# Cache rows of 32 KiB instead of 16 KiB: two heads per 4 MiB transfer, softmax and PV by pairs of heads

## The chip, the cores and the metric

One NeuronCore of a Trainium2 chip. The metric is the device time of one execution in microseconds (us), lower is better. Differences of less than 2% count as "same"; most comparisons are read from the traces and from several timed rounds on one chip, with the kernel before run beside each.

## The reference

One decode step: layernorm, attention of one query per batch row over a cache of 8,192 keys for 32 heads, and a feed-forward block, both added to x. Everything is bf16 in HBM.

```python
B, Sq, D = 4, 1, 512;  H, Sk, Dh = 32, 8192, 128;  F = 1792
def _A_ref(x, k_cache, v_cache, wq, wo):           # k_cache, v_cache: [B, H, Sk, Dh]
    q = (x @ wq).reshape(B, Sq, H, Dh).transpose(0, 2, 1, 3)
    scores = einsum("bhqd,bhkd->bhqk", q, k_cache) * (Dh ** -0.5)
    p = softmax(scores, axis=-1)
    o = einsum("bhqk,bhkd->bhqd", p, v_cache)
    return o.transpose(0, 2, 1, 3).reshape(B, Sq, H * Dh) @ wo
def _B_ref(x, w_gate, w_up, w_down):
    return (silu(x @ w_gate) * (x @ w_up)) @ w_down
xn = layernorm(A_x)
return A_x + _A_ref(xn, ...) + _B_ref(xn, ...)
```

K and V are 268 MB each, and each byte is used once. All else is small: 8 MB of projections, 5.5 MB of feed-forward weights.

## The kernel before

K and V come in tiles of 2 MiB, one per (head, batch row). A tile is [128 partitions x 8,192 elements]: partition p holds 64 consecutive keys, so a row of one partition is 16 KiB, contiguous in HBM. Nine buffers of 16 KiB per partition (`slot`) hold tiles of K, V and weights in turn. All loads are issued by SyncE, in program order.

```python
    T = Sk // P          # 64 keys on a partition
    NSLOT = 9
    LP = 4               # PV runs four tiles behind the scores
    nc.sync.dma_start(out=x_sb[:], in_=x_flat[:, :])
    ...                  # wq in two loads of 2 MiB
    def load_k(m):
        h, b = divmod(m, B)
        t_ = slot()
        nc.sync.dma_start(out=t_[:], in_=A_k_cache[b, h, :, :].rearrange("(p t) d -> p (t d)", p=P))
        k_tiles[m] = t_
    ...                  # load_v alike; the last V tile in 4 parts
    def load_wo(half):   # rows of 1 KiB, 16 of them on a partition
        n = H // 2
        t_ = slot()
        nc.sync.dma_start(out=t_[:].rearrange("p (h e) -> p h e", h=n),
                          in_=A_wo[half * n * P:(half + 1) * n * P, :].rearrange("(h p) e -> p h e", p=P))
```

Per K tile VectorE transposes four pieces of 16 keys per partition (laid out by the kernel in blocks of QB = 32 x 32 words), and TensorE takes each turned piece through four matmuls against a query matrix that is zero except in the right columns, so that all scores of a head gather in one PSUM tile of 128 rows x 512. After four tiles (one head) comes the softmax; PV runs for each V tile as 16 matmuls with 4 rows of output and 512 columns.

```python
    def t_piece(m, g):
        w = TG * Dh                                    # TG = 16
        kt = kt_pool.tile([P, w], dt.bfloat16, name="kt")
        src = k_tiles[m][:, g * w:(g + 1) * w].bitcast(dt.uint32)
        nc.vector.transpose(out=..., in_=src.rearrange("p (t j r) -> p t j r", j=2, r=QB))
    def s_piece(m, g):
        ...
        for jp in range(4):
            mm(s_ps[h][:], zq[h % 2][:, b, jp, off:off + P], kt[:, jp // 2, :, jp % 2], ...)
    def pv_chunk(m, k):
        mm(o_acc[h % 2][b * QB:b * QB + NV, :], pt[h][:, s * NV:(s + 1) * NV, 2 * (b * NTG + g)],
           v_tiles[m][:, k * 512:(k + 1) * 512], start=(k == 0))
    ...
    for i in range(M + LP + 1):                        # M = 128 tiles
        if i + 2 < M: load_k(i + 2)
        if 0 <= i + 2 - LP < M: load_v(i + 2 - LP, parts=4 if i + 2 - LP == M - 1 else 1)
        ...                                            # ffn and wo loads at fixed i
        for g in range(NTG): t_piece(i, g); s_piece(i, g)
        ...                                            # softmax, PV of tile i - LP, projection
```

Of the kernel before, what the change touches and what calls it, by code (L numbers as in the profile page):

```python
# [8 lines left out]
dt = mybir.dt  # L9
# [6 lines left out]
def kernel(  # L16
# [20 lines left out]
    assert D % P == 0 and F % P == 0 and Sk == 64 * P  # L37
# [3 lines left out]
    T = Sk // P  # L41
# [6 lines left out]
    NSLOT = 9  # L48
    LP = 4
# [34 lines left out]
    nc.sync.dma_start(out=x_sb[:], in_=x_flat[:, :])  # L84
    wq_v = A_wq.rearrange("(p c) n -> p c n", c=EC)
    wq_t = []
    for c2 in range(0, EC, 2):
        t_ = slot()
        nc.sync.dma_start(out=t_[:].rearrange("p (c n) -> p c n", c=2), in_=wq_v[:, c2:c2 + 2, :])  # L89
        wq_t.append(t_)  # L90
# [3 lines left out]
    def load_k(m):  # L94
        h, b = divmod(m, B)
        t_ = slot()
        nc.sync.dma_start(out=t_[:], in_=A_k_cache[b, h, :, :].rearrange("(p t) d -> p (t d)", p=P))  # L97
        k_tiles[m] = t_

    def load_v(m, parts=1):  # L100
        h, b = divmod(m, B)
        t_ = slot()
        src = A_v_cache[b, h, :, :].rearrange("(p t) d -> p (t d)", p=P)
        w = SLOT // parts
        for i in range(parts):
            nc.sync.dma_start(out=t_[:, i * w:(i + 1) * w], in_=src[:, i * w:(i + 1) * w])
        v_tiles[m] = t_
# [11 lines left out]
    zq = [const.tile([P, B, 4, ZW], dt.bfloat16, name=f"zq{i}") for i in range(2)]  # L119
# [5 lines left out]
    for o_ in o_acc:  # L125
# [4 lines left out]
    rowb = const.tile([P, B], dt.float32, name="rowb")  # L130
    nc.vector.reduce_sum(out=rowb[:], in_=ident_f[:].rearrange("p (a x g r) -> p x a g r", a=NQ, x=B, r=2)[:, :, :, :, 0],
                         axis=AX.XY)
    rowb_q = const.tile([P, B], dt.float32, name="rowb_q")
    nc.vector.tensor_scalar(out=rowb_q[:], in0=rowb[:], scalar1=qscale, scalar2=None, op0=ALU.mult)

# [29 lines left out]
    for c in range(EC):  # L165
        for half in range(NH):
            for cg in range(NQ):
                n0 = (c % 2) * H * Dh + (half * NQ + cg) * 512
                mm(q_ps[half][cg * QB:(cg + 1) * QB, :], xnt_w[:, c, :], wq_t[c // 2][:, n0:n0 + 512], start=(c == 0))
# [28 lines left out]
    def load_ffn():  # L198
        wg_t, wu_t, wd_t = slot(), slot(), slot()
        w = EC * F  # L200
        nc.sync.dma_start(out=wg_t[:, 0:w], in_=B_w_gate.rearrange("(p c) f -> p (c f)", c=EC))
        nc.sync.dma_start(out=wu_t[:, 0:w], in_=B_w_up.rearrange("(p c) f -> p (c f)", c=EC))
        nc.sync.dma_start(out=wd_t[:, 0:FC * D], in_=B_w_down.rearrange("(p c) e -> p (c e)", c=FC))
        ffn["w"] = (wg_t[:, 0:w].rearrange("p (c f) -> p c f", c=EC),
                    wu_t[:, 0:w].rearrange("p (c f) -> p c f", c=EC),
                    wd_t[:, 0:FC * D].rearrange("p (c e) -> p c e", c=FC))
# [26 lines left out]

    wo_t = []

    def load_wo(half):
        n = H // 2
        t_ = slot()
        nc.sync.dma_start(out=t_[:].rearrange("p (h e) -> p h e", h=n),
                          in_=A_wo[half * n * P:(half + 1) * n * P, :].rearrange("(h p) e -> p h e", p=P))  # L240
        wo_t.append(t_)


    kts, s_ps, pt, rcp, nmx, osb = {}, {}, {}, {}, {}, {}
    rs_t = {}

    def build_q(h):
        half, cg, hh = h // 16, (h % 16) // 4, h % 4
        for a in range(NQ):
            nc.vector.tensor_copy(  # L250
                out=zq[h % 2][a * QB:(a + 1) * QB, :, :, XO + a * QB].rearrange("p b (j r) -> p r j b", r=2),
                in_=qt[a * QB:(a + 1) * QB, half, :, hh * 2:hh * 2 + 2, cg * B:(cg + 1) * B])

    def t_piece(m, g):

        w = TG * Dh
        kt = kt_pool.tile([P, w], dt.bfloat16, name="kt")
        src = k_tiles[m][:, g * w:(g + 1) * w].bitcast(dt.uint32)
        nc.vector.transpose(out=kt[:].bitcast(dt.uint32).rearrange("p (j t r) -> p t j r", j=2, r=QB),  # L259
                            in_=src.rearrange("p (t j r) -> p t j r", j=2, r=QB))  # L260
        kts[m, g] = kt

    def s_piece(m, g):
        h, b = divmod(m, B)
        if b == 0 and g == 0:
            s_ps[h] = psS.tile([P, 512], dt.float32, name="sps")
        kt = kts.pop((m, g))[:].rearrange("p (j n r) -> p j n r", j=2, r=2)
        off = XO - 2 * (b * NTG + g)
        for jp in range(4):
            mm(s_ps[h][:], zq[h % 2][:, b, jp, off:off + P], kt[:, jp // 2, :, jp % 2],  # L270
               start=(b == 0 and g == 0 and jp == 0))

    def max_1(h):
        mx = small.tile([P, 1], dt.float32, name="mx")
        nc.vector.reduce_max(out=mx[:], in_=s_ps[h][:], axis=AX.X)  # L275
        nmx[h] = mx

    def max_2(h):

        mps = psM.tile([P, 512], dt.float32, name="mps")  # L280
        nc.tensor.matmul(mps[:, 0:P], lhsT=nmx.pop(h)[:, 0:1].to_broadcast([P, P]), rhs=ident_f[:, :],  # L281
                         is_transpose=True, start=True, stop=True, skip_group_check=True)
        nm = small.tile([P, B], dt.float32, name="nm")
        nc.vector.tensor_reduce(out=nm[:], in_=mps[:, 0:P].rearrange("p (a x g r) -> p x a g r", a=NQ, x=B, r=2)[:, :, :, :, 0],  # L284
                                axis=AX.XY, op=ALU.max, negate=True)
        nc.vector.tensor_tensor(out=nm[:], in0=nm[:], in1=rowb_q[:], op=ALU.mult)
        nb = small.tile([P, 1], dt.float32, name="nb")
        nc.vector.reduce_sum(out=nb[:], in_=nm[:], axis=AX.X)
        p_ = pp.tile([P, 512], dt.bfloat16, name="p_")
        rs = small.tile([P, 1], dt.float32, name="rs")  # L290
        nc.scalar.activation(out=p_[:], in_=s_ps.pop(h)[:], func=ACT.Exp, bias=nb[:, 0:1], scale=qscale,
                             accum_out=rs[:])
        pt[h] = p_
        rs_t[h] = (rs, mps)

    def pt_turn(h):
        t_ = pp.tile([P, TG, QB], dt.bfloat16, name="pt_")
        nc.vector.transpose(out=t_[:].rearrange("p t x -> p (t x)"), in_=pt[h][:])  # L298
        pt[h] = t_

    def row_sums(h):
        rs, mps = rs_t.pop(h)
        mm(mps[:, P:P + B], rs[:, 0:1].to_broadcast([P, P]), rowb[:], start=True)
        r_ = small.tile([P, B], dt.float32, name="rcp")
        nc.vector.reciprocal(out=r_[:], in_=mps[:, P:P + B])  # L305
        rcp[h] = r_

    def pv_chunk(m, k):
        h, b = divmod(m, B)
        g, s = divmod(k, TG // NV)  # L310
        mm(o_acc[h % 2][b * QB:b * QB + NV, :], pt[h][:, s * NV:(s + 1) * NV, 2 * (b * NTG + g)],
           v_tiles[m][:, k * 512:(k + 1) * 512], start=(k == 0))

    def fin_1(h):
        o_sb = pp.tile([P, 512], dt.float32, name="o_sb")
        nc.scalar.copy(out=o_sb[:], in_=o_acc[h % 2][:])  # L316
        osb[h] = o_sb

    def fin_2(h, nb=B):

        o_sb = osb.pop(h)
        xps = psX.tile([P, B], dt.float32, name="xps")
        for u in range(NV):
            mm(xps[:, 0:nb], o_sb[:, u * Dh:(u + 1) * Dh], ident_f[:, u:nb * QB:QB], start=(u == 0))
        return xps

    def fin_3(h, xps):
        nc.vector.tensor_tensor(out=otn[:, h, :], in0=xps[:], in1=rcp.pop(h)[:], op=ALU.mult)  # L328

    def pv_last(xps):  # L330

        h, b = divmod(M - 1, B)
        for t in range(T):
            g, u = divmod(t, TG)
            mm(xps[:, b:b + 1], v_tiles[M - 1][:, t * Dh:(t + 1) * Dh], pt[h][:, u, 2 * (b * NTG + g):2 * (b * NTG + g) + 1],
               start=False)

    def wo_mm(h):
        w = wo_t[h // (H // 2)][:].rearrange("p (h e) -> p h e", e=D)
        for j in range(2):  # L340
            mm(yo_ps[j][0:B, :], otn[:, h, :], w[:, h % (H // 2), j * DH:(j + 1) * DH], start=False)

    NK = T // NV
    R_FFN, R_WO = 9, M - 10
    wo_next, wo_ready = 0, 0
    build_q(0)
    for i in range(M + LP + 1):

        if i + 2 < M:
            load_k(i + 2)  # L350
        if 0 <= i + 2 - LP < M:
            load_v(i + 2 - LP, parts=4 if i + 2 - LP == M - 1 else 1)
# [4 lines left out]
        if i == R_WO - 3:  # L357
            load_wo(0)
        if i == R_WO - 2:
            load_wo(1)  # L360
        hs, bs = divmod(i, B)
        hp = hs - 1
        if i < M:
            for g in range(NTG):
                t_piece(i, g)
                s_piece(i, g)
                if g == 0 and bs == 0 and hp >= 0:
                    pt_turn(hp)
            if bs == B - 2 and hs + 1 < H:
                build_q(hs + 1)  # L370
            if bs == B - 1:
                max_1(hs)
        elif i == M:
            pt_turn(H - 1)
        mp = i - LP
        if mp == M - 1:
            xps = fin_2(H - 1, B - 1)
            pv_last(xps)
            fin_3(H - 1, xps)
            wo_ready = H  # L380
        elif 0 <= mp < M:
            for k in range(NK):
                pv_chunk(mp, k)
                if k == NK // 2 and i < M and bs == B - 1:
                    max_2(hs)
            hv, bv = divmod(mp, B)
# [55 lines left out]
```

## Time and profile before

| | before |
|---|---|
| time, median of 3 runs | 1296.54 us (1296.42 to 1296.56) |
| span in the profile | 1294.7 us |
| DMA, mean over the span | 426 GB/s of 551.5 MB |
| steady rate, 520 to 720 us | 431 GB/s |
| TensorE, VectorE busy | 84%, 54% |
| VectorE idle, waiting for K | 287 us |

A high busy share of TensorE beside a DMA that is always busy is not a contradiction: the kernel has two nearly full resources.

### The profile page before, as it was taken

The numbers are of one execution on the slowest core, as the hardware profiler recorded it, in microseconds if no ns is written. First come the engines' busy times: TensorE is split into PE (matmuls) and PEld (weight loads), VectorE is DVE, ScalarE is ACT, GpSimd is POOL, SyncE is SP. The second block draws the span as 40 slices with busy tenths as digits, with TensorE's granted clock in tenths as the row PEclk, the third lists the DMA queues.
The fourth block names the chain that finished last, engine by engine and source line by source line (L and its number), as shares of the span: only waits on it lengthen the run. The fifth ranks groups of instructions, "written<-read, shape, count | busy, mean of one in ns | idle before, by whom it ended". The sixth has DMA issues, their size and how long they took to land.

```text
span 1294.7 us, 11411 instructions
## 1 busy us (share of the span) xinstructions
PE 1091.8 (84%) x4758; PEld 425.8 (33%) x4758; DVE 693.1 (54%) x887; ACT 48.9 (4%) x103; POOL 5.6 (0%) x11
## 2 busy tenths in 40 slices
PE   5888888888888888887888888888888888886997
PEld 2343333333333333333333333333333333332333
DVE  7635554564555565555555555555555545543552
ACT  1000000000000000000000000000000000000000
POOL 1000000000000000000000000000000000000000
PEclk9999998999999999999999899998999999998999
DMA  9999999999999999999999999999999999999997
GB/s 395 431 429 430 431 429 432 430 431 430 432 431 429 430 431 432 429 430 431 432 430 429 431 432 431 430 431 431 430 431 431 430 430 431 431 402 420 430 432 321
DMA packets 42219, 551.51 MB, mean 426 GB/s; under 512 B 4268, under 2 KB 8376, under 8 KB 8888
## 3 DMA queue, kind: packets, MB, share of 16 engines
q1 hardware_dynamic: 42160, 550.79, 99.7%
q8 instruction: 37, 0.61, 0.2%
q14 instruction: 14, 0.11, 0.0%
q10 hardware_dynamic: 8, 0.00, 0.0%
HBM read 550.77 MB, written 0.00 MB: 425 GB/s over the span
## 4 chain that ended last, share of the span: by engine, by line
DMA 89%; PE 8%; DVE 3%; issue 0%; SPq 0%; ACT 0%; DVEq 0%; ACTq 0%
DMA slot<-in_A_k_cache_dram 86%; PE sps L74 4%; PE oacc L74 3%; DMA slot<-in_A_v_cache_dram 3%; DVE kt L259 3%; PE xps L74 0%; SPq L97 0%; PE mps L281 0%; PE mps L74 0%; SPq L89 0%; DVE otn L328 0%; ACT o_sb L316 0%; DVE pt__4838 L298 0%; DVE pt__6510 L298 0%; DVE pt__4014 L298 0%
## 5 line engine op out<-in xcount | busy, mean ns | idle before, releaser
L259 DVE STREAM_TRANSPOSE kt<-slot 128x1024 uint32<-128x1024 uint32 x512 | 593.5, 1212 | 287.2 <-DMA slot<-in_A_k_cache_dram 287.0
L74 PE MATMUL sps<-kt,zq 128*128 128x512 bf16 x2048 | 569.6, 413 | 181.3 <-DVE kt L259 167.4
L74 PEld LDWEIGHTS <-zq 128*128 128x128 bf16 x2048 | 208.0, 102 | 531.3 <-issue 358.9
L305 DVE RECIPROCAL rcp<-mps 128x4 f32<-128x4 f32 x32 | 5.8, 183 | 162.1 <-PE mps L74 162.1
L275 DVE TENSOR_REDUCE mx<-sps 128x1 f32<-128x512 f32 x32 | 22.1, 692 | 43.0 <-PE sps L74 43.0
L284 DVE TENSOR_REDUCE nm<-mps 128x4 f32<-128x64 f32 x32 | 7.2, 224 | 50.0 <-PE mps L281 50.0
L74 PE MATMUL xps<-ident_f,o_sb 128*128 128x4 f32 (+1 forms) x256 | 33.1, 253 | 0.7 <-ACT o_sb L316 0.7
L74 PEld LDWEIGHTS xps<-ident_f,o_sb 128*128 128x128 f32 x256 | 31.1, 192 | 1.2 <-ACT o_sb L316 1.2
L250 DVE COPY zq<-qt 32x16 bf16<-32x16 bf16 x128 | 23.5, 183 | 1.3
L328 DVE TENSOR_TENSOR otn<-xps,rcp 128x4 bf16<-128x4 f32 x32 | 5.2, 162 | 33.1 <-PE xps L74 33.1
L316 ACT COPY o_sb<-oacc 128x512 f32<-128x512 f32 x32 | 18.8, 586 | 18.0 <-PE oacc L74 17.8
L74 PE MATMUL oacc<-slot,pt__3190 128*4 128x512 bf16 x64 | 14.6, 379 | 0.2 <-DMA slot<-in_A_v_cache_dram 0.2
L74 PE MATMUL oacc<-slot,pt__5662 128*4 128x512 bf16 x64 | 14.6, 379 | 0.1
L74 PE MATMUL oacc<-slot,pt__1336 128*4 128x512 bf16 x64 | 14.6, 379 | 0.0
L74 PE MATMUL oacc<-slot,pt__372 128*4 128x512 bf16 x64 | 14.6, 379 | 0.0
L74 PE MATMUL oacc<-slot,pt__2572 128*4 128x512 bf16 x64 | 14.6, 379 | 0.0
L74 PE MATMUL oacc<-slot,pt__3602 128*4 128x512 bf16 x64 | 14.6, 379 | 0.0
L74 PE MATMUL oacc<-slot,pt__4632 128*4 128x512 bf16 x64 | 14.6, 379 | 0.0
L74 PE MATMUL oacc<-slot,pt__5456 128*4 128x512 bf16 x64 | 14.6, 379 | 0.0
L74 PE MATMUL oacc<-slot,pt__6754 128*4 128x512 bf16 x64 | 14.6, 379 | 0.0
L74 PE MATMUL oacc<-slot,pt__578 128*4 128x512 bf16 x64 | 14.6, 379 | 0.0
L74 PE MATMUL oacc<-slot,pt__1954 128*4 128x512 bf16 x64 | 14.6, 379 | 0.0
(206 smaller groups left out, 639.6 us busy)
## 6 DMA issues: line engine op xcount, KB each, us to landing
slot<-in_A_k_cache_dram SPq DMA_DIRECT2D x128, 2048.0 KB, 37.8
slot<-in_A_v_cache_dram SPq DMA_DIRECT2D x127, 2048.0 KB, 38.8
slot<-in_A_wq_dram SPq DMA_DIRECT2D x2, 2048.0 KB, 9.6
slot<-in_A_wo_dram SPq DMA_DIRECT2D x2, 2048.0 KB, 29.4
slot<-in_A_v_cache_dram SPq DMA_DIRECT2D x4, 512.0 KB, 28.0
slot<-in_B_w_gate_dram SPq DMA_DIRECT2D x1, 1792.0 KB, 35.1
slot<-in_B_w_up_dram SPq DMA_DIRECT2D x1, 1792.0 KB, 34.3
slot<-in_B_w_down_dram SPq DMA_DIRECT2D x1, 1792.0 KB
```

The source lines that it names most:

```text
L74: nc.tensor.matmul(out_ap, lhsT=lhsT, rhs=rhs, start=start, stop=True, skip_group_check=True, **kw)
L250: nc.vector.tensor_copy(out=zq[h % 2][a * QB:(a + 1) * QB, :, :, XO + a * QB].rearrange("p b (j r) -> p r j b", r=2), in_=qt[a * QB:(a + 1 ...
L259: nc.vector.transpose(out=kt[:].bitcast(dt.uint32).rearrange("p (j t r) -> p t j r", j=2, r=QB), in_=src.rearrange("p (t j r) -> p t j r", ...
L275: nc.vector.reduce_max(out=mx[:], in_=s_ps[h][:], axis=AX.X)
L284: nc.vector.tensor_reduce(out=nm[:], in_=mps[:, 0:P].rearrange("p (a x g r) -> p x a g r", a=NQ, x=B, r=2)[:, :, :, :, 0], axis=AX.XY, op= ...
L305: nc.vector.reciprocal(out=r_[:], in_=mps[:, P:P + B])
L316: nc.scalar.copy(out=o_sb[:], in_=o_acc[h % 2][:])
L328: nc.vector.tensor_tensor(out=otn[:, h, :], in0=xps[:], in1=rcp.pop(h)[:], op=ALU.mult)
```

## The change

The intent is to halve the number of packets for the same bytes. A tile becomes two heads of one batch row: each head lies on 64 partitions with 128 keys each, so a partition's row is 32 KiB and a transfer 4 MiB. There are five buffers of 32 KiB instead of nine of 16 KiB. Softmax is now done for two tiles (two heads, two batch rows) at a time, and PV covers both heads in one matmul with 8 rows of output; the weights of the half that does not belong to a head are zeros. Besides: wq comes in one load, wo as seven blocks with rows of 4 KiB and one with rows of 1 KiB, x comes on ScalarE's queue, and the last two V tiles are cut into 4 and 5 pieces so that less work is left after the last byte.

```diff
-    T = Sk // P
+    HT = 2
+    NT = M // HT
+    T = HT * Sk // P
-    NSLOT = 9
-    LP = 4
+    NSLOT = 5
+    LP = 2
...
-    nc.sync.dma_start(out=x_sb[:], in_=x_flat[:, :])
+    nc.scalar.dma_start(out=x_sb[:], in_=x_flat[:, :])
+    wq_t = slot()
+    nc.sync.dma_start(out=wq_t[:], in_=A_wq.rearrange("(p c) n -> p (c n)", c=EC))
...
-        nc.sync.dma_start(out=t_[:], in_=A_k_cache[b, h, :, :].rearrange("(p t) d -> p (t d)", p=P))
+        nc.sync.dma_start(out=t_[:], in_=A_k_cache[b, j * HT:(j + 1) * HT, :, :].rearrange("h (p t) d -> (h p) (t d)", t=T))
...   # load_v alike, with a list of widths
+        n = (NB4 - 1) * 4
+        nc.sync.dma_start(out=t_[:, 0:n * D].rearrange("p (k c e) -> p k (c e)", c=4, e=D),
+                          in_=A_wo[0:n * P, :].rearrange("(k p c) e -> p k (c e)", p=P, c=4))
+        nc.sync.dma_start(out=t_[:, n * D:H * D].rearrange("p (h e) -> p h e", e=D),
+                          in_=A_wo[n * P:H * P, :].rearrange("(h p) e -> p h e", p=P))
...   # softmax by groups of two tiles; probabilities of the two heads turned into ptz, zero elsewhere
+        mm(o_acc[j % 2][b * QB:b * QB + w, :], pt[n // 2][:, off:off + (w - 1) * QB + 1:QB],
+           v_tiles[n][:, k * 512:(k + 1) * 512], start=(k == 0))
...   # fin_1: a masking product and a reduce on VectorE replace four matmuls; fin_q fits wo's 4 KiB rows
-            load_v(i + 2 - LP, parts=4 if i + 2 - LP == M - 1 else 1)
+            load_v(nv, (32, 32, 32, 16, 16) if nv == NT - 1 else (32,) * 4 if nv == NT - 2 else (T,))
...
+            xps = x_tile()
+            pv_last(xps, range(T // 2))
+            fin_2(H // HT - 1, xps, nb=B - 1, start=False)
+            pv_last(xps, range(T // 2, T))
```

## The prediction

The 435.0 GB/s comes from the trace's packet records, and the 45 ns of step 1 from that and the steady 431 GB/s.

> **What bounds the kernel now.** The kernel streams 550.8 MB of K cache, V cache and weights from HBM once, so I read first what the DMA does over the span, then what the chain that ended last is made of. From the page:
>
> ```profile
> DMA  9999999999999999999999999999999999999997
> GB/s 395 431 429 430 431 429 432 430 431 430 432 431 429 430 431 432 429 430 431 432 430 429 431 432 431 430 431 431 430 431 431 430 430 431 431 402 420 430 432 321
> DMA packets 42219, 551.51 MB, mean 426 GB/s; under 512 B 4268, under 2 KB 8376, under 8 KB 8888
> DMA 89%; PE 8%; DVE 3%; issue 0%; SPq 0%; ACT 0%; DVEq 0%; ACTq 0%
> L259 DVE STREAM_TRANSPOSE kt<-slot 128x1024 uint32<-128x1024 uint32 x512 | 593.5, 1212 | 287.2 <-DMA slot<-in_A_k_cache_dram 287.0
> slot<-in_A_k_cache_dram SPq DMA_DIRECT2D x128, 2048.0 KB, 37.8
> ```
>
> The DMA is busy in every slice, the rate is flat at 429 to 432, and 89% of the chain is transfers. VectorE, which turns every K tile, is idle 287 us waiting for K to land: it follows the stream. A 2 MiB load takes 37.8 us from issue to landing, nearly eight times the 4.87 us that it takes alone at 431 GB/s: the queue is seven to eight loads deep. The stream itself is the bound, and only its own overhead, its start and its tail can be shortened. Next, busy time by stretches (columns: length, PE, weight loads, DVE, ACT, POOL, clock, DMA share, GB/s):
>
> ```profile
> 520.00:720.00 200.00, 168.59 (x704) 64.61 (x703) 110.28 (x140) 7.86 (x18) 0.00 (x0) 0.97 1.01 431
> 1150.00:1180.00 30.00, 23.20 (x93) 9.09 (x92) 11.42 (x16) 0.00 (x0) 0.00 (x0) 0.89 1.00 389
> 1280.00:1290.00 10.00, 8.70 (x65) 4.06 (x65) 0.16 (x1) 0.59 (x1) 0.00 (x0) 1.00 0.67 275
> ```
>
> 431 GB/s in the steady part; 389 over 30 us where the output projection's weights (wo, rows of 1 KiB) come in, which costs 30 x 42 / 431 = 2.9 us; a thin end. The issuing queue's timeline around wo shows an issue that is itself held up, which no other part of the steady stream has:
>
> ```profile
> 1127.67 0.39 SPq L239 DMA_DIRECT2D slot<-in_A_wo_dram  x1
> 1131.53 29.59 SPq L97 DMA_DIRECT2D slot<-in_A_k_cache_dram  x1
> 1161.21 0.38 SPq L106 DMA_DIRECT2D slot<-in_A_v_cache_dram  x1
> ```
>
> The K load behind wo takes 29.59 us to issue instead of 0.33, so the queue runs dry for a moment near 1160. Last, the end of the chain:
>
> ```profile
> 1251.38 32.79 DMA slot<-in_A_v_cache_dram
> 1284.17 0.04 issue
> 1284.21 3.63 PE oacc L74 x16
> ...
> 1287.92 0.59 ACT o_sb L316
> 1288.51 0.04 issue
> 1288.56 2.67 PE xps L74 x72
> ```
>
> The last V tile but one lands at 1284.17; then come its PV, the copy, the gather and the last tile's 64 matmuls, ending at 1291.22. The trace's packet records put the last V packet at 1288.8, so the tail after the last byte is 1294.7 - 1288.8 = 5.9 us, because PV of the tile before holds it up.
>
> [...] Its single packet records have medians of 611 ns for 16,384 B, 535 for 14,336 B, 159 for 4,096 B, 46 for 1,024 B and 9 for the 4-byte completion writes. The first four lie on one line: (611 - 46) / (16,384 - 1,024) is 27.19 B per ns, times 16 engines 435.0 GB/s, plus 8.3 ns per packet. [...]
>
> **The change part by part.**
> 1. K, V and the query weights come in 4 MiB transfers of 128 rows of 32 KiB, each engine moving 8 packets for twice the bytes. At 431 GB/s 2 MiB take 4.866 us, at 435.0 they would take 4.821: 45 ns of overhead per 2 MiB for 8 packets and a completion write. (Their records sum to 8 x 8.3 + 9 = 75 ns; consecutive packets overlap a little, so I trust the elapsed figure.) Both halve, to 22 ns per 2 MiB. There are 128 K, 128 V and 2 query loads: 258 x 22.4 ns = 5.8 us saved.
> 2. wo comes as 7 blocks of 4 KiB rows and one of 1 KiB rows: 56 x 159 + 32 x 46 ns = 10.4 us per engine, against 4 MiB at 431 GB/s of 9.7, so 0.7 us is lost instead of 2.9. The queue then holds about 90 descriptors of wo instead of 256 for each half, and I expect no held issue. 2.2 us saved.
> 3. The last two V tiles are cut into 4 and 5 pieces with rows of 8 and 4 KiB; this costs about 0.2 us back.
> 4. x goes to ScalarE's queue, so the first big load is issued one 0.4 us slot earlier: 0.35 us saved.
> 5. Tail: PV of the tile before the last is done as its pieces land, more than 5 us before the end; behind the last piece remain 16 of the 128 closing matmuls. From the rows here: 0.3 landing, 16 x 27 ns = 0.45, product 0.17, four wo matmuls 0.65, cast 0.36, output 2.4, joints 0.1: 4.4 us against 5.9. 1.4 us saved.
> 6. Compute moves but stays off the path. The K transposes and score matmuls keep number and shape (512 and 2,048). PV keeps its 512-column matmuls (127 x 16 = 2,032 become 63 x 32 = 2,016), now with 8 rows of output instead of 4, half of them unused cross terms of the two heads. Per 4 MiB K tile VectorE does 8 x 1.19 = 9.5 us; per two tiles 4 copies, max, four short softmax steps and two half-height transposes, about 3.9; per four tiles a masking product and a reduce, about 1.9 by the 0.69 us of a 512-column reduce. Four tiles: 38 + 7.8 + 1.9 = 48 us in a period of 4 x 19.4 = 78 us, 62% against 55% now. TensorE: 32 x 0.28 + 32 x 0.227 = 16.3 us of 19.4.
>
> Sum: 5.8 + 2.2 - 0.2 + 0.35 + 1.4 = 9.6 us. The span goes from 1294.7 to 1285.1; the time is 1.8 us above the span, so 1286.9.
>
> **The rivals.**
> - The stream starves. Nine slots of 2 MiB become five of 4 MiB, so fewer, larger loads are ahead. By the build's issue order a V load waits for the K tile two before the one last asked for to be turned, a K load for the PV of the V tile five loads back. If K lands at t, its turning ends at t + 9.7 and the V load goes out with K, V, K (29 us) still queued; PV of the V that landed at t + 9.7 ends near t + 17.5 and frees the next K load with some 31 us queued. With wo holding a slot the depth falls to about 19 us. Against it: the 37.8 us depth of today needs only one transfer to cover. If I have misread an order, each miss costs a few us per tile, and 64 tile pairs could make 2 to 5%: 1320 or more.
> - Overhead goes with bytes, or a 32 KiB row is cut into two packets. Against it: the straight line from 1 to 16 KiB. Then step 1 gives under 1.5 us, and the time is about 1291.
> - Compute becomes the bound. The matmuls that project the attention output run 8 heads per iteration near the end, 4.4 us on TensorE beside 16.3 in 19.4; it lags 1 to 2 us an iteration for four iterations, inside the queue's depth. Worth under 2 us.
> - 32 KiB rows reach or pass another ceiling. The whole stream at 435.0 GB/s is 550.8 MB / 435.0 = 1266 us; with 2.2 us of start and 4.4 of tail and the 1.8 outside the span this is about 1274.5, only 1.7% better. So 2% is out of reach unless the line's slope is not the ceiling.
>
> **Range and chances.** The sum's terms are each good to about a third, some 3 us; the rivals on the slow side add 4 to 5. The range is 1282 to 1292.5. Faster by over 2% (below 1270.6) would need more than the measured ceiling: 0.02. Slower by over 2% needs starving: 0.04. Within 2%: 0.94.
>
> **What would show it.** Step 1: packets of 32,768 B at about 1214 ns and a steady rate of 433 GB/s; 431 would make it wrong. Step 2: no dip below about 415 where wo arrives and no issue of tens of us. Step 5: under 5 us from the last V packet to the end. Step 6 and the first rival: the DMA busy in every slice and VectorE still waiting for K; slices below 425 in the middle, or a K or V load issued with under one transfer queued, would make the prediction wrong.

## More of the kernel before

One more part of the page became useful later, the DMA queues (queue and kind: packets, MB, share of the 16 engines' time):

```profile
q8 instruction: 37, 0.61, 0.2%
q14 instruction: 14, 0.11, 0.0%
```

The reader is to see that the 16 DMA engines carry not only the kernel's data but also blocks of the engines' own instructions: 37 packets of 16 KiB on q8, which over TensorE's 4,758 matmuls and 4,758 weight loads is about 64 bytes for each, and 14 of 8 KiB on q14.

## The result

The changed kernel takes 1288.95 us, median of 4 runs (1288.89 to 1289.28); the kernel before, in the same rounds, 1296.53. The ratio is 0.9942, with a 95% interval of 0.9925 to 0.9959. A ratio here is the mean time of one kernel's runs over that of the other's of the same rounds, so it is not quite the ratio of the medians quoted. It is 0.6% faster, "same" by the 2% rule, inside the predicted range and 2 us slower than the predicted time. The span went from 1294.7 to 1287.1 us, so the 1.8 us outside it stayed. The granted TensorE clock is a little lower (0.933, before 0.958). No run varies the clock alone; experiment 9 ran as fast at 0.767, but with 43% of the matmuls left out.

From the page of the changed kernel, the lines that answer to those shown of before:

```profile
DMA  9999999999999999999999999999999999999997
GB/s 407 427 430 435 437 425 437 429 436 431 432 435 428 436 432 433 431 432 435 431 435 428 434 432 431 436 431 433 430 434 431 437 430 432 433 431 427 433 434 304
DMA packets 21529, 551.49 MB, mean 428 GB/s; under 512 B 2268, under 2 KB 2792, under 8 KB 3944
DMA 50%; PE 31%; DVE 14%; issue 5%; ACT 1%; SPq 0%; DVEq 0%
L277 DVE STREAM_TRANSPOSE kt<-slot 128x1024 uint32<-128x1024 uint32 x512 | 587.6, 1210 | 90.4 <-DMA slot<-in_A_k_cache_dram 89.5
slot<-in_A_k_cache_dram SPq DMA_DIRECT2D x64, 4096.0 KB, 39.2
```

The packets are halved, the DMA is still busy in every slice, and no slice in the middle is below 425. The dip at the output projection's weights (402 before) is nearly gone (427). Issue to landing stays near 39 us, now four transfers of 9.7 us instead of eight of 4.9. But the chain that ended last is only half transfers, against 89%, and VectorE's wait for K fell from 287.0 to 89.5 us. This is the first thing that I had not weighed enough: the rate is unchanged, yet the computation runs much closer to the stream.

The windows (length, PE, weight loads, DVE, ACT, POOL, clock, DMA share, GB/s) of the changed kernel:

```profile
520.00:720.00 200.00, 170.83 (x712) 66.72 (x711) 116.74 (x150) 5.65 (x13) 0.00 (x0) 0.91 1.00 433
1150.00:1180.00 30.00, 27.44 (x109) 10.46 (x108) 19.17 (x25) 0.57 (x1) 0.00 (x0) 0.92 1.01 426
1270.00:1280.00 10.00, 10.00 (x108) 5.24 (x106) 1.40 (x3) 0.59 (x1) 0.00 (x0) 1.00 0.78 327
1280.00:1290.00 10.00, 3.35 (x74) 2.42 (x70) 1.09 (x3) 0.36 (x1) 0.00 (x0) 0.61 0.08 31
```

433 where 431 stood, 426 where 389 stood. New is the third row: from 1270 to 1280, while the queue still holds work, the DMA engines are busy only 78% of the time (before, this stretch had 1.01 and 434). Some engines have run out of work while others still have some. The issuing queue around wo:

```profile
1144.00 0.39 SPq L253 DMA_DIRECT2D slot<-in_A_wo_dram  x1
1144.43 17.27 SPq L255 DMA_DIRECT2D slot<-in_A_wo_dram  x1
1161.80 13.99 SPq L95 DMA_DIRECT2D slot<-in_A_k_cache_dram  x1
```

Issues are still held, for 17.27 and 13.99 us; the prediction had expected none. Last, the end of the chain:

```profile
1265.54 17.13 DMA slot<-in_A_v_cache_dram
...
1282.71 0.60 PE xps L76 x16
...
1283.34 0.18 DVE otn L366
...
1283.56 1.03 PE yo_ps L76 x4
...
1284.61 0.36 ACT res L458
```

The last V piece landed at 1282.67, then 16 of the closing matmuls, the product, four projection matmuls, the cast and 2.1 us of writing the output: the tail by the design.

The trace's packet records allow a finer account (a record is one packet; the cadence is the median distance of one load's completion from the next, over 1,000 us). The last row is how long before the last packet the first DMA engine ran out of work.

| from the packet records, us | before | after | difference |
|---|---|---|---|
| first packet of wq | 2.145 | 1.774 | -0.37 |
| from there to the end of the last V packet (the stream) | 1286.67 | 1280.59 | -6.08 |
| last packet to end of span | 5.84 | 4.74 | -1.09 |
| sum (span) | 1294.66 | 1287.11 | -7.55 |
| cadence of 4 MiB | 2 x 4.862 | 9.681 | -0.043 |
| a full row's packet, median | 0.611 | 1.213 | |
| first engine idle before the last packet | 3.4 | 7.7 | +4.3 |

### The profile page after: what moved, and what is told of

It reads as the page before. It is cut to its first block, busy times and chain, and to the rows that moved or that the text cites. A ratio compares the mean times of both kernels' runs of the same rounds, so it can differ in the third digit from the quotient of the medians.

```text
span 1287.1 us, 11189 instructions
## 1 busy us (share of the span) xinstructions
PE 1083.1 (84%) x4778; PEld 430.3 (33%) x4778; DVE 738.1 (57%) x951; ACT 39.7 (3%) x87; POOL 5.3 (0%) x13
## 2 busy tenths in 40 slices
DMA packets 21529, 551.49 MB, mean 428 GB/s; under 512 B 2268, under 2 KB 2792, under 8 KB 3944
## 4 chain that ended last, share of the span: by engine, by line
DMA 50%; PE 31%; DVE 14%; issue 5%; ACT 1%; SPq 0%; DVEq 0%
DMA slot<-in_A_k_cache_dram 44%; PE oacc L76 17%; PE sps L76 12%; DVE kt L277 11%; DMA slot<-in_A_v_cache_dram 6%; PE mps L76 1%; DVE ptz L318 1%; DVE o L356 1%; PE xps L76 1%; DVE o_sb L354 1%; ACT o_sb L353 0%; PE mps L299 0%; DVE otn L377 0%; PE yo_ps L76 0%; DVE rcp L328 0%
## 5 line engine op out<-in xcount | busy, mean ns | idle before, releaser
L277 DVE STREAM_TRANSPOSE kt<-slot 128x1024 uint32<-128x1024 uint32 x512 | 587.6, 1210 | 90.4 <-DMA slot<-in_A_k_cache_dram 89.5
L76 PE MATMUL oacc<-slot,ptz 128*8 128x512 bf16 x2016 | 450.4, 379 | 0.4 <-DMA slot<-in_A_v_cache_dram 0.4
L76 PEld LDWEIGHTS <-ptz 128*8 128x8 bf16 x2016 | 177.5, 92 | 258.1 <-issue 27.8
L354 DVE TENSOR_TENSOR o_sb<-o_sb,rowu 128x512 f32<-128x512 f32 x16 | 11.1, 693 | 89.2 <-ACT o_sb L353 89.0
L76 PE MATMUL xps<-rowy,o 128*32 128x4 f32 (+1 forms) x228 | 13.5, 205 | 37.3 <-DVE o L356 37.3
L76 PEld LDWEIGHTS xps<-rowy,o 128*32 128x32 f32 (+1 forms) x228 | 12.1, 154 | 44.9 <-DVE o L356 44.9
L268 DVE COPY zq<-qt 32x8 bf16<-32x8 bf16 x128 | 21.3, 166 | 1.3
L356 DVE TENSOR_REDUCE o<-o_sb 128x128 f32<-128x512 f32 x16 | 16.3, 1020 | 0.5
L76 PEld LDWEIGHTS <-slot 128*128 128x128 bf16 x272 | 11.7, 126 | 3.5 <-DVE slot L188 2.6
L76 PE MATMUL mps<-rowb,rs 128*128 128x4 f32 x64 | 12.3, 263 | 0.0
L299 PE MATMUL mps<-ident_f,mx 128*128 128x128 f32 x32 | 10.3, 323 | 0.8 <-DVE mx L293 0.8
```

The lines of the kernel that those rows point to most:

```text
L76: nc.tensor.matmul(out_ap, lhsT=lhsT, rhs=rhs, start=start, stop=True, skip_group_check=True, **kw)
L268: nc.vector.tensor_copy(out=zq[gr % 2][a * QB:(a + 1) * QB, :, :, XO + a * QB].rearrange("p b (j r) -> p r j b", r=2), in_=qt[a * QB:(a + ...
L277: nc.vector.transpose(out=kt[:].bitcast(dt.uint32).rearrange("p (j t r) -> p t j r", j=2, r=QB), in_=src.rearrange("p (t j r) -> p t j r", ...
L299: nc.tensor.matmul(mps[:, 0:P], lhsT=nmx.pop(gr)[:, 0:1].to_broadcast([P, P]), rhs=ident_f[:, :], is_transpose=True, start=True, stop=True ...
L354: nc.vector.tensor_tensor(out=o_sb[:], in0=o_sb[:], in1=rowu[:].unsqueeze(2).to_broadcast([P, NV, Dh]), op=ALU.mult)
L356: nc.vector.reduce_sum(out=o1[:], in_=o_sb[:].rearrange("p u d -> p d u"), axis=AX.X)
```

## The experiments

All kernels below start from the changed one, unless it is said otherwise; "+3.0" means 3.0 us over its 1288.95. The kernel before took 1296.48 to 1296.59 beside all of them. Results were correct in all runs by the comparison with the reference; the ninth was wrong on purpose, and still passed.

The first four take back one part of the change each.

**1. 16 KiB packets in 4 MiB transfers.** A gap of 64 bytes in the middle of each row of the buffers, so that a row arrives as two packets (37,657 in all, 21,529 in the changed kernel).

```diff
+    GAP = 32
+    HS = SLOT // 2
-        return slots.tile([P, SLOT], dt.bfloat16, name="slot")
+        return slots.tile([P, SLOT + 2 * GAP], dt.bfloat16, name="slot")
+        nc.sync.dma_start(out=t_[:].rearrange("p (c w) -> p c w", c=2)[:, :, 0:HS], in_=src.rearrange("q (c w) -> q c w", c=2))
...   # the transposes and PV skip the gap
```

> The changed kernel with a 64-byte gap in the middle of every K and V tile in SBUF, so that the transfers stay 4 MiB each but every row arrives as two packets of 16 KiB. The completion records of the two traces give a steady cadence of 4.862 us per 2 MiB before and 9.681 per 4 MiB after, so 41 and 39 ns over the 435 GB/s of the packet line, each for 8 packets and one completion. My theory, that the saving is one of packets: 8 more packets per tile and engine at some 4.5 ns each make the cadence 9.717 us, and 126 tiles make +4.5 us: about 1293.5 us. Rival one, that the saving is one of transfers (fewer, larger ones): no change, 1289. Rival two, that the whole saving was wo and the tail: no change, 1289.

It took 1299.66 us in 5 rounds (ratio to the kernel before 1.0024, 1.0011 to 1.0038), +10.7.

```profile
DMA packets 37657, 551.49 MB, mean 425 GB/s; under 512 B 2268, under 2 KB 2792, under 8 KB 3944
520.00:720.00 200.00, 171.52 (x709) 67.05 (x707) 114.23 (x147) 6.43 (x15) 0.00 (x0) 0.90 1.01 429
```

The steady rate fell from 433 to 429, below the 431 of before. The cadence is 9.749 us for 4 MiB, against 9.681 for the changed kernel and an expected 9.717. So the direction is that of the packets, but the size is more than they can account for: nearly half of these packets took 612 ns or more, where 611 is the median before. (68 ns more per tile over 126 whole tiles is 8.6 us; the stream grew by 10.6, and I can't place the other 2.)

**2. The same packets from two loads.** Each tile as two loads of 2 MiB with plain rows of 16 KiB.

```diff
+        for c in range(2):
+            nc.sync.dma_start(out=t_[:, c * SLOT // 2:(c + 1) * SLOT // 2], in_=src[:, c * SLOT // 2:(c + 1) * SLOT // 2])
...   # load_v alike; the last two V tiles as they were
```

> The changed kernel with every K and V load issued as two loads of 2 MiB, halves of the rows: 16 KiB packets and twice the completions, the transfers of the kernel before in the structure of the changed one. My theory: all of the 21.5 ns per 2 MiB comes back, cadence 4.862 us, +5.4 us, about 1294.3 us. If the run with the gap stays at 1289 and this one is slower, it is the transfer and not the packet. Rival two (wo and tail did it all): 1289.

It took 1295.70 us in 5 rounds (0.9994, 0.9981 to 1.0006), +6.75.

```profile
520.00:720.00 200.00, 172.16 (x710) 67.38 (x711) 118.50 (x152) 5.07 (x12) 0.00 (x0) 0.90 1.01 431
```

The cadence is 4.862 us per 2 MiB, exactly that of the kernel before, and the steady rate is back at 431. The stream is 1286.09 us, 5.5 longer than the changed kernel's: 43 ns x 126 tiles is 5.4. Everything else of the change is in this kernel, and the rate of before is back: this shows that the gain of the stream comes from the rows' length (and the halved completion writes of 4 bytes that go with it: 2,268 packets under 512 B in the changed kernel, 4,284 here), and sizes it. This run also doubles the number of loads; that the number of loads alone makes the difference does not fit experiment 1, whose loads stayed 4 MiB and were slow all the same. The remaining 1.5 us of its time lie behind the last cast: from there to the end of the span 3.6 us passed instead of 2.1, which is the output's transfer. I did not look into that.

**3. wo in rows of 1 KiB.** One transfer of 4,096 rows; the last stages use the plain projection for all heads.

```diff
-        n = (NB4 - 1) * 4
-        nc.sync.dma_start(out=t_[:, 0:n * D].rearrange(...), in_=A_wo[0:n * P, :].rearrange(...))
+        n = 0
-    JL = H // HT - 2
+    JL = 0
```

> The changed kernel with wo loaded as before, 4,096 rows of 1 KiB, here in one transfer, and the attention output laid out to fit. By the prediction's step 2: 2.2 us slower, 1291.2. By the packet records alone (46 against 159/4 ns per KiB): +1.4 us, 1290.4. A rival from the trace: the 16 engines drift apart (8 us between the first and the last to finish the stream in the changed kernel, 3.5 us before), and a queue that runs dry behind wo lets them close up again, so that the end comes nearer: then the cost is smaller than 1.4 us or nothing, and the first engine goes idle less than 5 us before the last packet instead of 8.

It took 1289.93 us in 5 rounds (1289.62 to 1291.34; 0.9951), only +0.98 by the medians; single runs lie 0.7 to 2.4 above, their spans 0.7 to 1.5 above the 1287.1 of the changed kernel. The page's rates and the issuing queue (start, us, what):

```profile
GB/s 407 434 426 431 440 431 430 434 430 436 429 434 430 432 436 432 432 433 431 435 430 435 430 433 434 430 434 431 435 430 433 433 431 436 428 434 394 427 438 323
```

```profile
1157.57 23.56 SPq L95 DMA_DIRECT2D slot<-in_A_k_cache_dram  x1
```

The loss at wo is all there: a slice of 394 and a K load held for 23.56 us. Yet the time rose by under half of the 2.2 us that the slice's loss is worth. The packet records show where the rest went: here the first engine ran out 3.45 us before the last packet, not 7.7. While wo loads, each engine is idle 1.46 us on average (0.14 in the changed kernel, which is only the stops described in experiment 6; 1.11 in the kernel before), because the queue behind wo runs dry; engines that were ahead wait there for those behind, and start level again. Without the dry spell they stay apart, and the difference is paid at the end of the stream. That was the rival written down for this run, and both its numbers, the time and the spread at the end, came out its way. So wo's longer rows are worth about 1 us, not 2.2. (The kernel also needs the plain projection for every head, which goes with the layout; its tail, 4.81 us, is that of the changed kernel within 0.1.)

**4. The last two V tiles whole.**

```diff
-            load_v(nv, (32, 32, 32, 16, 16) if nv == NT - 1 else (32,) * 4 if nv == NT - 2 else (T,))
+            load_v(nv)
```

> The changed kernel with its last two V tiles loaded whole instead of in 4 and 5 pieces. Step 5 of the prediction, that the pieces shorten the tail: 128 closing matmuls of 27 ns instead of 16 stand behind the last packet, +3.0 us, and up to 1 us more if PV of the tile before (7.3 us after its landing, and 2.5 us of copy, mask and reduce) is late: 1292 to 1293 us, 7.5 to 8.5 us from the last V packet to the end instead of 4.7. Rival: the tail is hidden by the drift of the engines, because most of the tile before has landed long before; then the time changes by under 1 us.

It took 1291.99 us in 5 rounds (0.9965), +3.0. The end of its chain:

```profile
1254.06 28.36 DMA slot<-in_A_v_cache_dram
...
1282.46 3.98 PE xps L76 x130
```

The stream ended 0.2 us earlier (1280.36 long), as step 3 had it, and the tail after the last packet was 8.17 us instead of 4.74: all 128 closing matmuls (3.98 us in the chain) stand behind the last byte instead of 16 of them (0.60). The cut is worth 3.0 us in this kernel, of which 1.1 are a gain over before, since before cut its last tile too.

The rest asks two questions which these four left open.

**5. Why was the gap dearer than its packets?** The same as experiment 1 with a gap of 128 bytes, to tell an offset of 64 bytes from the form of the transfer (two runs per row).

```diff
-    GAP = 32
+    GAP = 64
```

> The run with 16 KiB packets in 4 MiB transfers again, with a gap of 128 bytes in the tile instead of 64. The first such run was slower than my theory (cadence 9.749 us per tile instead of 9.717): its trace has half of its packets at 612 to 618 ns instead of 611, and starts 607 ns apart only for the other half. I think that the second halves, written at an offset of 64 bytes, are the slow ones. Then here all packets take 611 ns, start 607 apart, and the cadence is 16 x 607 + 6 = 9.718 us, 37 ns over the changed kernel's 9.681: 126 x 37 ns = +4.7 us, 1293.6 us. Rival: it is the form of the transfer (two runs per row), not the offset: 9.749 us and 1299.7 us again.

1297.99 us in 3 rounds (1.0011, 0.9996 to 1.0026), +9.0, at a cadence of 9.744 us. A quarter of the packets still took 614 to 619 ns. So the offset has a part (nearly half of the packets were slow with 64 bytes, and the time was 1.7 us longer), but not the whole: at either gap a transfer with two runs per row costs some 20 to 25 ns more per 4 MiB than two transfers with one. Why, the records don't say. A larger gap, of 256 bytes for instance, was not run, so an effect of alignment is not excluded; the gap also lengthens each slot, and so moves where the slots start.

**6. Do fetches of instructions drive the engines apart?** In the packet records the engines fall behind one another in steps of about 1.4 us, at the times of the 16 KiB packets on q8 (each takes about 0.93 us), and of about 0.8 us at those of q14. If so, more fetches would make the end more ragged. To 56 tiles I added 40 matmuls of one column into an unused column of PSUM.

```diff
+        if R_FFN < i < NT - 2:
+            for _ in range(40):
+                mm(yo_t[0][0:1, 400:401], ident[:, 0:1], ident[:, 0:1], start=False)
```

> The changed kernel with 40 one-column matmuls more per tile into an unused column, in 56 of the 64 tiles: 2,240 matmuls and weight loads, 4,480 instructions of 64 bytes, 17.5 more packets of 16 KiB on the instruction queue (37 in both traces, whose instructions of TensorE number 9,556 x 64 bytes = 37 x 16 KiB). In the trace each such packet stops one data engine for 1.4 us, and their times repeat with a period of eight. My theory of the drift: the fetches hit the same half of the 16 engines, so these end the stream late: +17.5 / 8 x 1.42 = +3.1 us, about 1292 us, and the first engine goes idle some 11 us before the last packet instead of 7.7. If the fetches are spread over all 16: +1.5 us and the drift as before. If fetches cost the stream nothing: 1289. TensorE itself gets 1.1 us more per tile of 19.4, which its slack of 3 covers.

1292.64 us in 3 rounds (0.9971), +3.7, in two parts. The stream grew by 2.4 us, with 18 more fetches (the line below); the tail grew by 1.2, because TensorE came late to the end. The first engine ran out 8.4 us before the last packet: more than 7.7, far less than the 11 expected (the end of the next section has the reason).

```profile
q8 instruction: 55, 0.90, 0.2%
```

**7. Can the load be evened out?** If the engines that lag get fewer bytes, the stream should end level. One K tile was cut; the intent was to give half of the engines more of it.

```diff
+        cuts = (0, 96, 104, 112, 120, P) if n == 40 else (0, P)
+        for r0, r1 in zip(cuts, cuts[1:]):
+            nc.sync.dma_start(out=t_[r0:r1, :], in_=src[r0:r1, :])
```

> The changed kernel with one K tile, number 40 of 64, cut into a load of 96 rows and four of 8 rows. [...] If the engines that end late are among 8 to 15: the stream ends 2.4 us earlier, about 1286.6 us, faster than both kernels, and the first engine goes idle 3 us before the last packet. If late engines are among 0 to 7: 2.4 us later, 1291.4 us, and the first goes idle 12 us before. If the engine of a row is not what I think: 1289.

It took 1313.63 us in 3 rounds (1.0136), +24.7, a failure from which little on the question follows. Its windows:

```profile
780.00:800.00 20.00, 13.90 (x45) 4.54 (x44) 8.41 (x14) 0.78 (x2) 0.00 (x0) 0.83 1.05 210
800.00:820.00 20.00, 3.80 (x18) 1.54 (x17) 0.60 (x1) 0.00 (x0) 0.00 (x0) 0.66 0.97 247
```

For some 36 us the DMA was "busy" at half the rate, with packets of 2 to 4 us instead of 1.21. The packet records show two parts. First come the packets of the load of 96 rows, six on each of the 16 engines, at 2.5 to 2.9 us each (medians by engine); then the four loads of 8 rows, each on eight engines, at 2.3 to 3.7 us a packet. (The page has 2,300 packets under 512 B, 32 more than in the changed kernel, as four loads with 8 completion writes each would make.) So the packets of the large load took twice as long as usual too, although it ran on all 16 engines. Why either load was slow, no run shows. Note how the busy share hides it: 1.05 at 210 GB/s.

**8. More fetches, early.** As experiment 6, but 56 matmuls in tiles 6 to 45 only, to leave the last tiles alone.

```diff
+        if R_FFN < i < 46:
+            for _ in range(56):
```

> The run with more fetches again, with the 2,240 one-column matmuls in tiles 6 to 45 (56 each) so that TensorE is not behind at the end: in the first such run the tail after the last V packet had grown by 1.2 us beside the 2.4 us of the stream. If fetches lengthen the stream: about 55 packets on the instruction queue, the stream again about 2.4 us longer than the changed kernel's, the tail back at 4.7 us, 1291.3 us. If the first run's loss was TensorE being late: 1289.

1291.95 us in 3 rounds (0.9965), +3.0; again 55 packets on q8. The stream is 1283.08 us, +2.5, which repeats experiment 6. The tail is +0.6, and the first engine ran out 7.95 us before the end. So more of TensorE's fetches do lengthen the stream, by some 0.14 us each, though the end is hardly more ragged.

**9. Fewer fetches.** Every second score and PV matmul is left out; the attention is wrong. (The comparison still called it correct within its tolerance, so that comparison would not catch an error of this kind.)

```diff
-        for jp in range(4):
+        for jp in range(0, 4, 2):
...
-                pv_chunk(npv, k)
+                if k % 2 == 0:
+                    pv_chunk(npv, k)
```

> The changed kernel with every second score matmul and every second PV matmul left out, so with a WRONG RESULT on purpose: 2,032 matmuls and as many weight loads less, 4,064 instructions, 15.9 of the 37 instruction packets. All loads stay. If fetches lengthen the stream by 2.4 us per 18: 2.1 us less, about 1286.8 us, and the first engine goes idle about 4 to 5 us before the last packet instead of 7.7. If TensorE's work or the fetches have no part in the stream: 1289 and 7.7 us.

1288.77 us in 3 rounds (0.9940), no change. The stream is 1280.56 us (1280.59 with all matmuls), with 21 packets on q8 instead of 37, and the first engine again ran out 7.7 us before the end; now one engine alone lags, in steps of 0.8 us. The expected shortening failed, but not for want of an effect: 2.5 us before the last packet 9 engines are still busy in the changed kernel and only that one here, so the others did end earlier.

```profile
DMA 77%; DVE 11%; PE 7%; issue 5%; SPq 0%; ACT 0%; DVEq 0%
```

Its chain is 77% transfers. That is worth having for the other question: with TensorE's work cut from 84% of the span to 57%, the time did not move, so TensorE's 31% of the chain in the changed kernel cost nothing.

**10. More of VectorE's instructions.** Five memsets of one element after each transpose in tiles 6 to 45, 1,600 in all, to add fetches on q14.

```diff
+                if R_FFN < i < 46:
+                    for _ in range(5):
+                        nc.vector.memset(junk[:], 0.0)
```

> The changed kernel with five one-element memsets on VectorE after every transpose of tiles 6 to 45: 1,600 instructions of 0.06 us or so, none of which anything waits for. VectorE goes from 9.7 to some 12 us of 19.4 per tile. The run with fewer fetches for TensorE did not get faster: in its trace one engine alone falls behind in steps of 0.8 us, at the times of the 8 KiB packets of the second instruction queue (12 of them, about what VectorE's, ScalarE's and SyncE's 1,180 instructions make), while the others stay within 3 us. My theory now: those packets all go to one data engine, which is the last in the changed kernel too. Then 1,600 x 64 bytes / 8 KiB = 12.5 more packets, 12.5 x 0.8 = +10 us on that engine, the stream up to 10 us longer, about 1298 us. If they are spread over the engines, or the last engine is late for another reason: under +1.5 us, 1290. If only VectorE's work counts, which is off the path: 1289.

1352.72 us in 3 rounds (1350.94 to 1354.36; 1.0429): the kernel is now bound by computation, and the run says nothing of fetches. One line from its waits (engine, line and what it waited for: us in total, times, longest) and three from its timeline (start, us):

```profile
PE sps L76 <- DVE junk L410: 169.3, 244, 1.5
```

```profile
703.27 1.07 PE L76 MATMUL sps<-kt,zq 128*128 128x512 bf16 x4 [0.23 <-DVE junk L410]
...
708.21 1.06 PE L76 MATMUL sps<-kt,zq 128*128 128x512 bf16 x4 [0.58 <-DVE junk L410]
709.20 7.08 PE L76 MATMUL oacc<-slot,ptz 128*8 128x512 bf16 x32
```

The second of these groups of four score matmuls is the third after the first: one starts every (708.21 - 703.27) / 3 = 1.65 us, paced by VectorE; PV of another tile follows only when all eight groups are done. 8 x 1.65 + 7.3 is 20.5 us a tile (an estimate from these rows), more than the 19.4 that a K and a V tile take to load. The measured cost, 63.8 us over 40 tiles, is 1.6 us a tile, so 21.0. This is a result, if not the one that I was after: the order of the instructions makes VectorE's turning and TensorE's PV follow one another.

**11. Fewer of VectorE's instructions.** K turned in four pieces of double length, in two buffers of 8 KiB.

```diff
+        if g % 2:
+            return
+        kt = kt_pool.tile([P, 2 * w], dt.bfloat16, name="kt")
+        src = k_tiles[n][:, g * w:(g + 2) * w].bitcast(dt.uint32)
```

> The changed kernel with K turned in four pieces of twice the length per tile instead of eight (two buffers of 8 KiB instead of five of 4 KiB): 256 instructions less on VectorE, two packets of 8 KiB less. My theory now: 1.6 us less on the engine that ends last; TensorE's fetches then hold the end at some 0.5 to 1.5 us less than in the changed kernel, about 1288 us, a little faster than both kernels. If instruction packets play no part: 1289, or slower, if two buffers of kt are too few and VectorE falls behind the stream.

1292.60 us in 3 rounds (1290.26 to 1294.28; 0.9968), +3.6. The stream is 0.4 us shorter (1280.20), the tail 3.5 longer (8.22 us): TensorE comes late to the end, where the chain is now its PV (12.01 us up to 1281.84) and not a transfer. That the coarser pieces make it late is likely, but not shown. No gain.

**12. More of ScalarE's instructions.** 80 copies of one element in every second tile from 7 to 45.

```diff
+        if R_FFN < i < 46 and bb == 1:
+            for _ in range(80):
+                nc.scalar.copy(out=junk[:, 0:1], in_=junk[:, 1:2])
```

> The changed kernel with 80 one-element copies on ScalarE at the end of every second tile from 7 to 45, 1,600 instructions that nothing waits for, on an engine that is busy 3% of the time: some 16 us of ScalarE after its last work of a pair of tiles, of 36 us in which it has none. The run with memsets on VectorE did not tell what it was for, because VectorE's memsets held up TensorE's score matmuls and the kernel became bound by compute. Here no engine on the path is touched. Theory: the 8 KiB instruction packets all go to one data engine, and that engine ends last: 12.5 packets more, 12.5 x 0.8 = +10 us, the stream up to 10 us longer, about 1298 us. If they are spread over the engines, or another engine is the last: under +1.5 us, 1290. If instruction packets do nothing: 1289.

1288.82 us in 3 rounds (0.9939), no change, though the small fetches doubled from 12 (12 packets of 8 KiB for 1,600 instructions are 61 bytes each):

```profile
q14 instruction: 24, 0.20, 0.0%
```

The stream is 1280.71 us, and the first engine ran out 7.7 us before the end. What falls with this is the theory that all fetches of 8 KiB go to one DMA engine, the one that ends last. The new ones went elsewhere: 4 us before the last packet 10 engines are still busy, 9 in the changed kernel.

No run beat the changed kernel: experiments 9 and 12 stand within 0.2 us of it, and 9 computes something else.

## Why the prediction was right, and where not

The stream as the bound, the mechanism (a fixed cost per packet, about 4.3 ns) and the verdict were right; the predicted 9.6 us are 7.6 in fact. By the prediction's own steps:

| step | predicted, us | measured, us | from |
|---|---|---|---|
| 1 rows of 32 KiB | -5.8 | -5.5 | experiment 2, stream |
| 2 wo in longer rows | -2.2 | -1.0 | experiment 3 |
| 3 cut V tiles | +0.2 | +0.2 | experiment 4, stream |
| 4 x on ScalarE's queue | -0.35 | -0.37 | first packet, before and after |
| 5 tail | -1.4 | -1.1 | last packet to end, before and after |
| sum | -9.6 | -7.8 | measured together: -7.6 |

**Step 1** holds to 0.3 us. The packets of 32 KiB took 1,213 ns (predicted 1,214), the cadence fell by 21.5 ns per 2 MiB (predicted 22.4), and the rate in the middle is 433. The caution to take the elapsed time and not the sum of the records was needed: records put 8.3 ns on a packet, but from one packet's start to the next on an engine it is 607 ns for 16 KiB and 1,209 to 1,210 for 32 KiB, which is about 4.3 ns over the bytes at 435.0 GB/s.

**Step 2** is the term that was mis-sized: 1.0 us instead of 2.2. Its observation was right (a dip from 431 to 389, and now 426), but it took the whole dip for a loss. Experiment 3 brought the dip back, at 394, and cost 1.0 us, because a queue that runs dry also lets engines that lag catch up; without it the lag is paid at the end, where the first engine now stops 7.7 us before the last instead of 3.4. (Its 256 descriptors "for each half" of wo are those of both halves together: the trace of before has 4,100 packets of 1 KiB, of which wo's 4,096 rows make 256 for each of the 16 engines.) Its second claim, "I expect no held issue", was wrong: 17.27 and 13.99 us. That fewer descriptors would end the holding was my inference; what holds an issue, no run shows. The held issues no longer made the queue run dry (from 20 to 1,265 us the only gaps between an engine's packets over 60 ns are those at fetches of instructions), so they cost nothing that I can find.

**Step 5** was right in kind, and 0.3 us off: 4.74 us, of which the four projection matmuls took 1.03 and not 0.65, and the output 2.1 and not 2.4. Experiment 4 confirms that the cut does it.

**Step 6** was right that the computation stays off the path, and too generous about the room that it leaves. TensorE's sum is as predicted. The timeline of the changed kernel (start, us; in brackets idle before and its releaser):

```profile
699.64 9.11 DVE L277 STREAM_TRANSPOSE kt<-slot 128x1024 uint32<-128x1024 uint32 x8
700.92 8.95 PE L76 MATMUL sps<-kt,zq 128*128 128x512 bf16 x32 [1.42 <-DVE kt L277]
709.79 1.25 PE L76 MATMUL oacc<-slot,ptz 128*8 128x512 bf16 x5
...
711.23 6.00 PE L76 MATMUL oacc<-slot,ptz 128*8 128x512 bf16 x27
...
717.49 1.25 DVE L277 STREAM_TRANSPOSE kt<-slot 128x1024 uint32<-128x1024 uint32 x1 [5.54 <-DMA slot<-in_A_k_cache_dram]
```

8.95 + 1.25 + 6.00 is 16.2 us, the 16.3 of the prediction. But shares of 62% and 84% hide that the two engines' work is in one loop: turning 8 x 1.2 = 9.7, then PV 7.3, leaves about 2.4 of 19.4 us (an estimate from these rows and the cadence). Experiment 10 went past that and lost 1.6 us a tile; experiment 9 took work away and gained nothing. Both together say: not the bound, with little to spare. The reduce that gathers PV's output took 1.02 us, not the 0.69 assumed, without effect.

**The rivals.** "Starves" is out: no K or V load was issued late enough to empty the queue, and the depth stayed near 39 us. "Overhead goes with bytes" is out by experiment 2. "Another ceiling" is out at this size: the stream kept the slope of 435.0 GB/s. "Compute becomes the bound" is out, by experiment 9.

**What drives the engines apart, and what stays open.** The engines end up to 7.7 us apart, and experiments 6, 9 and 12 alone don't say why: eighteen more fetches of TensorE's lengthened the stream by 2.4 and 2.5 us, twice; sixteen fewer did not shorten it, twelve more of ScalarE's did not lengthen it. The packet records do say it. A record doesn't name its DMA engine, but an engine's packets follow one another without a gap of over 60 ns, so that all 16 can be followed, up to where each has moved 29 MB (near 1,075 us), and the stop that a fetch makes can be seen on the engine that it hits:

| engines | stops by q8, by q14 | behind the first engine, us |
|---|---|---|
| changed kernel: seven | 0, 0 to 2 | 0 to 1.2 |
| eight | 3 to 5, 0 | 4.5 to 7.4 |
| one | 0, 8 | 7.1 |
| experiment 9: seven | 0, 0 to 2 | 0 to 1.2 |
| eight | 2 to 3, 0 to 1 | 2.9 to 4.0 |
| one | 0, 7 | 5.7 |

At 1.42 us for a stop by q8 and 0.84 for one by q14, their sum gives the lag of every engine in both runs within 0.7 us. So the fetches do drive the engines apart: TensorE's go to eight engines in turn, most of those on q14 to one other. Experiment 9 brought the eight nearer and left the one, which then set the end alone; no run took stops from both. In experiments 6 and 8 the engines came to wo 8.8 us apart (7.3 in the changed kernel), and there the leading ones waited (0.4 and 0.6 us, averaged over all 16), which levelled them again. Open is what assigns a fetch to a DMA engine.

## What to carry to other kernels

Where the stream is the bound, as here, what was left to gain was the cost per packet (5.5 us), the start (0.37) and the tail (1.1): work them out from the elapsed time per load and not from the packets' own records, which overlap (611 ns long, 607 from start to start). A dip in the rate was not all loss here (2.2 us predicted from the rates at wo, 1.0 in the time of experiment 3): ask whether it lets the laggards catch up, and look at when the first engine runs out as well as the last. The fetches of instructions alone set the engines here some 7 us apart, about as much as the whole change gained. And when tiles get larger, add up the loop that one tile goes through on several engines; shares of each engine alone (57% and 84% here) don't tell how near the computation is to becoming the bound.
